# Attention followed by two MoE layers on one core: the products with V one slot later, and a unit's outputs in the softmax's tiles

## The chip, the cores and the metric

The kernel runs on one core of one Trainium2 chip. The metric is device microseconds of that core for one execution of the whole program, the median of several runs. The core's engines each work through their own list of instructions in order: PE (matrix products, into the PSUM accumulators), DVE (vector operations), ACT (activation functions and copies), POOL (a second, slower vector engine) and SP (which here only issues DMAs). Semaphores hold an instruction back until what it reads is there and what it overwrites is no longer needed.

## The reference

```python
scores = scale * np.matmul(q, k.transpose(0, 1, 3, 2))        # 4 batches, 8 heads, 576 x 576, head size 64
...
h = np.maximum(x @ w1 + b1, 0.0)                              # x[i, j] = log1p(|i - j|) / log1p(max(i, 1))
bias = h @ w2                                                 # one 576 x 576 table for each head
scores = scores + bias.transpose(2, 0, 1)[None, :, :, :]
scores = scores - np.max(scores, axis=-1, keepdims=True)
attn = np.exp(scores)
attn = attn / (np.sum(attn, axis=-1, keepdims=True) + 1e-09)
return np.matmul(attn, v).astype(np.float32)
...
h = np.maximum(np.maximum(x @ w1, x @ w2), x @ w3)            # first MoE: 2304 tokens, 512 -> 768
return (h @ w_out).astype(np.float32)                         # 768 -> 512
...
g = np.where(pos, h, np.where(neg, 0.0, (h + beta) ** 2 / (4.0 * beta)))   # second MoE: h = x @ w_in, 512 -> 2048
return (g @ w_out).astype(np.float32)                         # 2048 -> 512
```

## The kernel before

**Attention in slots.** The 576 query rows are cut into four blocks of 128 and a rest of 64. A *unit* is one block of one batch: eight heads, so eight *slots*; the rest block takes two heads at once and has four slots a unit. There are 20 units and 144 slots. Blocks 0, 1 and 2 come first, four units each (slots 0 to 95); then, for each batch, a unit of block 3 and one of the rest block (slots 96 to 143).

**One slot.** `emit_s` (L664) computes scores on PE, two slots together; the two tiles tagged `s` are PSUM. `emit_soft` takes them: DVE adds the bias table and finds the row maximum in one instruction (L678, into a tile tagged `sp`), ACT takes the exponential (L680, in place), ACT copies it to 16 bits (L696, the first half of a tile tagged `phl`), POOL computes what the rounding lost (L697 and L698, the second half), and a transposing DMA on SP's queue (L700) writes both halves, turned, into a tile tagged `pt`. `emit_pv` (L716 for the rest block, L720 otherwise) multiplies the turned probabilities with V, 14 products a slot, into the accumulator `pav`. (In the first two units every odd slot is turned on PE instead, L683 to L692.)

**The lag.** The main loop goes over slots i and emits the score of slot i + 1, the softmax of slot i and the product with V of slot i - LAG. LAG is read with `PRM.get("lag", 3)`.

**A unit's end.** After its last product `emit_norm` scales the accumulator by the sums (DVE L732, into `xf`, of which there is one), copies it to 16 bits (ACT L734, into `px`, of which there is one), computes the rest (POOL L735) and turns it by a DMA (L743) into `xT`, from which the first MoE layer reads. `xf` also serves the bias table's first part at the start (L410).

**Tiles.** `st(shape, type, tag)` gives the next tile of a tag's ring; a tag has the number of tiles that BUFS and `bufs` say (`sp` 4, `phl` 4, `pt` 4, `k` 5), and whoever gets a tile again waits for its last readers.

**What stands around it.** PE's other work fills the gaps between slots: the bias tables of the next blocks (L375 and L356), the first MoE layer (`mlp1` L775, three products of 12 matmuls for one of its columns, and `mlp2` L797), and sums that scale the weights (L454, L522). Everything is recorded with a priority, and a scheduler orders each engine's list from these priorities and from its own estimate of times; no list is written out by hand. After the last slot come the rest of the first MoE layer, and from about 660 us on the second one (L1007 and L1033, L1085 and L1124).

Of the kernel before, what the change touches and what calls it, by code (L numbers as in the profile page):

```python
# [7 lines left out]
F16 = mybir.dt.float16  # L8
BF16 = mybir.dt.bfloat16
F32 = mybir.dt.float32  # L10
# [10 lines left out]
def kernel(ctx: ExitStack, tc: tile.TileContext, qt, kt, vr, small, mw1, mw2, mw3, mwo, win, wo2, out):  # L21
# [8 lines left out]
    P = 128  # L30
    B, H, S, D = 4, 8, 576, 64
# [12 lines left out]
        ef=1,  # L44
        vl=[0, 0, 2, 11],
        vm=[0, 0, 8, 15],
        vs=[0, 0, 11, 19],
        wo=38,
        cm=[0, 3, 6, 9, 13, 16],
        veng='vv',  # L50
# [13 lines left out]
        look=4,  # L64
        xat=1,
        xs=12,
        bufs={'k': 5, 'pt': 4, 'xT': 2, 'phl': 4},
        xeng='vvvv',
        b1='vg',
        cs=8,  # L70
        cr=1,
    )
    WO, VENG, WENG, PENG, WARM, WARM2 = (PRM[k] for k in ("wo", "veng", "weng", "peng", "warm", "warm2"))
# [20 lines left out]
    def st(shape, dt, tag):  # L94
        return sb.tile(shape, dt, tag=tag, name=tag, bufs=BUFS.get(tag, 1))
# [69 lines left out]
    if True:  # L165
# [91 lines left out]
        for g in range(4):  # L257
            p = slice(32 * g, 32 * g + 32)
# [136 lines left out]
        def bias_pair(gq):  # L395

            pb = ps.tile([P, 2, 512], F32, tag="s", name="s", bufs=2)
            for c in range(2):
                m = st([P, 2 * S], F16, "phl")[:, :8 * P].rearrange("p (t i) -> p t i", t=8)
                w0 = rw[:, S - 4 * (8 * (gq + c) + 7):][:, 0:P]  # L400
                win_ = bass.AP(tensor=w0.tensor, offset=w0.offset, ap=[w0.ap[0], [4, 8], [1, P]])
                V.tensor_tensor(m, win_, thr[:, 0:P].unsqueeze(1).to_broadcast([P, 8, P]), ALU.is_gt)
                pbc = pb[:, c].rearrange("p (x q g) -> p x q g", x=16, q=8)
                for t in range(8):
                    for s in range(2):
                        T.matmul(pbc[:, :, 7 - t], m[:, t], coef[:, s].rearrange("p a h g -> p (a h) g"), start=(s == 0), stop=(s == 1))
            pbv = pb.rearrange("p c (a h k) -> p c a h k", a=2, h=H)
            k = slice(32 * gq, 32 * gq + 64)
            tmp = st([P, 512], F32, "xf").rearrange("p (c h k) -> p c h k", c=2, h=H)
            V.tensor_tensor(tmp, pbv[:, :, 0], xt0[:, k].rearrange("p (c k) -> p c k", c=2).unsqueeze(2).to_broadcast([P, 2, H, 32]), ALU.mult)  # L410
            for c in range(2):
                last_pair[0] = V.scalar_tensor_tensor(bias_sb[0][:, :, 32 * (gq + c):32 * (gq + c) + 32], pbv[:, c, 1], c_cs, tmp[:, c], ALU.mult, ALU.add)
# [312 lines left out]
        def emit_norm(u):  # L725
            n = u.n
            m = 64 * n
            rd = st([P, H, 1], F32, "rd")
            V.tensor_scalar(rd[:, :n, 0], u.sums[:, :n], 1e-9, None, ALU.add)
            V.reciprocal(rd[:, :n, 0], rd[:, :n, 0])  # L730
            xf = st([P, 512], F32, "xf")
            V.tensor_tensor(xf[:, :m].rearrange("p (h d) -> p h d", h=n), u.pav[:, :m].rearrange("p (h d) -> p h d", h=n), rd[:, :n].to_broadcast([P, n, 64]), ALU.mult)  # L732
            px = st([P, 1024], F16, "px")
            A.activation(px[:, :m], xf[:, :m], AF.Copy)  # L734
            G.tensor_tensor(px[:, m:2 * m], xf[:, :m], px[:, :m], ALU.subtract)  # L735
            key = (u.j, 0 if n == 4 else u.b // 2)
            if key not in xbox:
                xbox[key] = st([P, 2048], F16, "xT")
            if n == 4:
                d = xbox[key].rearrange("p (c b t) -> p c b t", c=4, b=B)[:, :, u.b]  # L740
            else:
                d = xbox[key].rearrange("p (c t) -> p c t", c=8)[:, :, P * (u.b % 2):P * (u.b % 2) + P]
            SP.dma_start_transpose(out=d, in_=px[:, :2 * m])  # L743
# [114 lines left out]
        for gq in range(0, 18, 2):  # L858
            bias_pair(gq)
            while conv_left and PRM["cm"][6 - len(conv_left)] <= gq - 18:  # L860
                conv_moe(conv_left.pop(0))
# [32 lines left out]
        for i in range(NS + LAG + 1):  # L894
# [15 lines left out]
            with sooner("norm"):  # L910
                while pend_norm:
                    emit_norm(pend_norm.pop(0))
# [51 lines left out]
        with sooner("norm"):  # L964
            while pend_norm:
                emit_norm(pend_norm.pop(0))
# [249 lines left out]
```

## Time and profile before

| | |
|---|---|
| median of 3 runs | 1042.64 us (1042.3 to 1043.9) |
| the profiled execution | 1048.62 us, of which the span of its instructions is 1046.9 us |
| mean granted clock of PE | 0.942 |
| busy share of the span | PE 90%, PE's weight loads 74%, DVE 68%, ACT 57%, POOL 48% |
| the chain that ended last | PE 51%, DVE 16%, DMA 12%, ACT 9%, POOL 5% |
| products with V | from 50.6 us to 583.2 us |

An idle engine costs time only where somebody waits for it. PE has the largest share, so its idle stretches, and what ended them, are the first thing to read; the trace puts in brackets how long an engine sat idle before an instruction and who released it. The granted clock is 1 at 2.4 GHz and one half at 1.2 GHz; a value between them is a mean over a stretch with both.

### The profile page before, as it was taken

Reading aid. Unit: us, or ns where it says so; the run is one execution under the profiler, and the core shown is the slowest. Engines: PE = TensorE matmul, PEld = TensorE weight load, DVE = VectorE, ACT = ScalarE, POOL = GpSimd, SP = SyncE. Lnnn points to the kernel's source line nnn. Section 1 sums busy time; section 2 is a strip of 40 time slices with the busy share of each in tenths; the row PEclk is TensorE's granted clock in tenths of the full one; section 3 lists DMA queues with packets and bytes.
Section 4 is the critical chain, followed back from the end, with each engine's and each line's share of the span. In section 5 each row is a group of like instructions: output and inputs, shape, how many; then the busy total and the mean of one; then the engine's idle time right before and its main releaser. Section 6 shows DMA issues by size and latency. Waiting matters only on the chain.

```text
span 1046.9 us, 25962 instructions
## 1 busy us (share of the span) xinstructions
PE 946.7 (90%) x10258; PEld 769.7 (74%) x10258; DVE 713.8 (68%) x1614; ACT 600.0 (57%) x1194; POOL 498.4 (48%) x721
## 2 busy tenths in 40 slices
PE   5669788898999999998899889989999999999993
PEld 5547667677888878877677768534588888888882
DVE  8977777776556678654455487598786677676662
ACT  4688874864565645777677677443344444344441
POOL 1012477665667764655455221986034344344340
PEclk7667889989999999999999899999999999999997
DMA  9795998998799988999999842010020010000000
GB/s 302 218 264 124 243 209 216 195 211 216 158 242 195 191 189 183 214 237 213 201 217 182 205 169 92 21 41 1 1 82 22 1 41 22 2 21 21 2 22 20
DMA packets 238910, 141.47 MB, mean 135 GB/s; under 512 B 187460, under 2 KB 217668, under 8 KB 238276
## 3 DMA queue, kind: packets, MB, share of 16 engines
q1 hardware_dynamic: 238788, 139.81, 57.0%
q8 instruction: 80, 1.31, 0.5%
q14 instruction: 42, 0.34, 0.1%
HBM read 79.68 MB, written 15.27 MB: 91 GB/s over the span
## 4 chain that ended last, share of the span: by engine, by line
PE 51%; DVE 16%; DMA 12%; ACT 9%; POOL 5%; issue 5%; SPq 1%; POOLq 0%; DVEq 0%; ACTq 0%
PE pm L1085 13%; PE pm L775 12%; PE s L1124 11%; DMA pt<-phl 5%; PE s L664 5%; PE pav L720 3%; PE s L1033 2%; PE pm L797 2%; POOL phl L698 2%; ACT sp L680 2%; DVE sp L678 2%; PE pm L375 1%; DMA x_d<-hl 1%; DMA ab<-in_moe_w_dram 1%; ACT phl L696 1%
## 5 line engine op out<-in xcount | busy, mean ns | idle before, releaser
L775 PE MATMUL pm<-xT,aw 128*128 128x256 f16 (+1 forms) x2160 | 246.6, 269 | 9.6 <-ACT hm L780 4.3
L775 PEld LDWEIGHTS <-aw 128*128 128x128 f16 x2160 | 194.0, 101 | 47.0 <-issue 25.4
L698 POOL TENSOR_TENSOR phl<-sp,phl 128x512 f16<-128x512 f32 x136 | 161.7, 1189 | 0.0
L680 ACT ACTIVATE sp<-sp,mx 128x576 f32<-128x576 f32 x144 | 110.6, 768 | 79.3 <-DVE mx L678 79.1
L664 PE MATMUL s<-k,qz 64*128 64x288 f32 (+1 forms) x576 | 134.8, 455 | 11.1 <-DVE mx L678 8.7
L697 POOL TENSOR_TENSOR phl<-sp,phl 128x64 f16<-128x64 f32 x136 | 48.4, 356 | 200.4 <-ACT phl L696 128.4
L1102 ACT ACTIVATE sp<-pm,vec 128x256 f32<-128x256 f32 x112 | 61.3, 556 | 93.5 <-PE pm L1085 93.4
L678 DVE CUSTOM_DVE_ANT_0 sp<-s,ab 128x576 f32<-128x576 f32 x128 | 93.7, 752 | 30.1 <-POOL phl L698 11.7
L720 PEld LDWEIGHTS <-pt 128*128 128x128 f16 x1792 | 75.9, 102 | 36.7 <-DMA pt<-phl 22.7
L664 PEld LDWEIGHTS s<-k,qz 64*128 64x128 f32 (+1 forms) x576 | 72.6, 198 | 33.2 <-DVE mx L678 13.0
L696 ACT ACTIVATE phl<-sp 128x576 f16<-128x576 f32 x136 | 89.9, 672 | 2.4 <-DMA pt<-phl 1.7
L720 PE MATMUL pav<-v,pt 128*128 128x64 f16 x1568 | 73.8, 198 | 17.6 <-DMA pt<-phl 15.8
L1085 PEld LDWEIGHTS <-ab 128*128 128x128 f16 x840 | 82.1, 98 | 10.3
L797 PE MATMUL pm<-hh,wo 128*128 128x256 f16 x648 | 78.4, 276 | 4.5 <-ACT hl L802 3.4
L1106 POOL TENSOR_TENSOR hh<-hh 128x128 f32<-128x128 f32 x56 | 30.3, 540 | 106.2 <-DVE hh L1104 101.3
L1103 DVE SCALAR_TENSOR_TENSOR hh<-pm,vec,sp 128x256 f32<-128x256 f32 x112 | 52.7, 478 | 34.3 <-ACT sp L1102 34.1
L797 PEld LDWEIGHTS <-wo 128*128 128x128 f16 x648 | 62.6, 99 | 15.3 <-issue 6.0
L787 POOL TENSOR_TENSOR hh<-hm,hh 128x256 f16<-128x256 f32 (+1 forms) x60 | 43.7, 728 | 63.3 <-ACT hh L786 62.0
L782 DVE SCALAR_TENSOR_TENSOR hm<-pm,hm 128x256 f32<-128x256 f32 (+1 forms) x120 | 47.1, 392 | 36.0 <-PE pm L775 19.1
L1124 PEld LDWEIGHTS <-xT 128*128 128x128 f16 x588 | 57.4, 98 | 7.8 <-ACT xT L1111 1.2
L1124 PEld LDWEIGHTS <-wo 128*128 128x128 f16 x588 | 57.5, 98 | 6.7
L1107 POOL TENSOR_TENSOR hh<-hh 128x128 f32<-128x128 f32 x56 | 25.8, 461 | 72.6 <-DVE hh L1104 67.9
(282 smaller groups left out, 1945.5 us busy)
## 6 DMA issues: line engine op xcount, KB each, us to landing
k<-in_k_dram SPq DMA_DIRECT2D x64, 288.0 KB, 4.1
v<-v_d SPq DMA_DIRECT2D x24, 640.0 KB, 4.9
ws<-in_moe_w_out_dram SPq DMA_DIRECT2D x15, 512.0 KB, 5.6
ws<-in_moe_w_in_dram SPq DMA_DIRECT2D x11, 512.0 KB, 4.4
x_d<-hl SPq DMA_DIRECT2D x36, 128.0 KB, 2.8
qz<-in_q_dram SPq DMA_DIRECT2D x16, 256.0 KB, 4.8
ab<-in_moe_w_dram SPq DMA_DIRECT2D x8, 512.0 KB, 8.8
qz<-x_d SPq DMA_DIRECT2D x4, 1024.0 KB, 4.8
```

The costliest lines, as they stand in the source:

```text
L664: last_score[0] = T.matmul(sbox[i + r][:, c, :288], q[p, s if u.j == SJ else s // 2], k[p, 288 * c:288 * c + 288], start=True, stop=True)
L678: V.tensor_tensor_reduce(halves(sn), sbox.pop(i)[:, :, :288], halves(bias_sb[u.j][:, h]), -0.125, 3e38, ALU.add, ALU.min, mx)
L680: last_soft[0] = A.activation(pf, sn, AF.Exp, scale=-1.0, bias=mx, accum_out=u.sums[:, h:h + 1])
L696: A.activation(hl[:, :S], pf, AF.Copy)
L698: G.tensor_tensor(hl[:, S + 64:], pf[:, :512], hl[:, :512], ALU.subtract)
L720: T.matmul(u.pav[:, 64 * h:64 * h + 64], pt[:, c], v[:, sl, 64 * (h % 4):64 * (h % 4) + 64], **kw)
L775: T.matmul(o, wm[:, ft, i, wp, kk], x_rhs(key, xp, kk) if n == 256 else x_rhs(key, xp, kk)[:, c], start=(x == 0), stop=(x == 11))
L797: T.matmul(pm, wo16[:, ft, wp, P * d:P * d + P], hh[:, ft, hp], start=(ft == 0 and y == 0), stop=(ft == NF1 - 1 and y == 2))
L1085: T.matmul(pm, w[:, wp, kk], x2t[ORDER[y]][:, kk, xp, 256 * sub:256 * sub + 256], start=(x == 0), stop=(x == 11))
L1102: A.activation(r, pm, AF.Relu, scale=c_ch[:, f], bias=c_half)
L1103: V.scalar_tensor_tensor(t, pm, c_c[:, f], r, ALU.mult, ALU.max)
L1124: T.matmul(m[x], gl[:, gp, i], w[:, wp], start=(start and z == 0 and x % 2 == 0), stop=(stop and z == 2 and (x % 2 == 1 or x == 6)))
```

## The change

The products with V are emitted four slots behind the softmax (`lag=4`). The ring of turned probabilities has five tiles instead of four, and so has `phl`. `xf` and `px` are gone: a unit's scaled outputs take the next `sp` tile, their 16-bit halves the next `phl` tile, and the bias table's first part takes an `sp` tile for its temporary. The split of batch 3's V (`vs`) moves from slot 19 to slot 20, since it overwrites what the product of slot 15 reads. No instruction is added or removed on any engine. A line of PRM is added, so every line after the 71st of the kernel before has a number that is greater by one.

```diff
-        vs=[0, 0, 11, 19],
+        vs=[0, 0, 11, 20],
...
-        bufs={'k': 5, 'pt': 4, 'xT': 2, 'phl': 4},
+        bufs={'k': 5, 'pt': 5, 'xT': 2, 'phl': 5},
...
         cs=8,
+        lag=4,
         cr=1,
...
-            tmp = st([P, 512], F32, "xf").rearrange("p (c h k) -> p c h k", c=2, h=H)
+            tmp = st([P, S], F32, "sp")[:, :512].rearrange("p (c h k) -> p c h k", c=2, h=H)
...
-            xf = st([P, 512], F32, "xf")
+            xf = st([P, S], F32, "sp")
...
-            px = st([P, 1024], F16, "px")
+            px = st([P, 2 * S], F16, "phl")
```

**PE, slot 124** (the first slot of block 3, batch 2). Before: the scores of slots 124 and 125 (`s_8862`, `s_8863`), then the products of slots 120 to 124, each shown by its first weight load (`pt_8670`, `pt_8728`, `pt_8784`, `pt_8876`, `pt_8940`), and the scores of slots 126 and 128 between them.

```order
L664 MATMUL s_8862<-k_8657,qz_67 128x288
L664 MATMUL s_8863<-k_8657,qz_67 128x288
...
L720 LDWEIGHTS pt_8670
...
L720 LDWEIGHTS pt_8728
...
L664 MATMUL s_8980<-k_8774,qz_67 128x288
...
L720 LDWEIGHTS pt_8784
...
L720 LDWEIGHTS pt_8876
...
L664 MATMUL s_9093<-k_8429,qz_67 128x288 x2
L720 LDWEIGHTS pt_8940
```

After: the scores of slots 124 and 125 (`s_8786`, `s_8787`), then the products of slots 119 to 124 (`pt_8529` to `pt_8868`), with the scores of slots 126 and 128 between them.

```order
L665 MATMUL s_8786<-k_8589,qz_67 128x288
L665 MATMUL s_8787<-k_8589,qz_67 128x288
...
L717 LDWEIGHTS pt_8529
...
L665 MATMUL s_8918<-k_8716,qz_67 128x288 x2
...
L721 LDWEIGHTS pt_8602
...
L721 LDWEIGHTS pt_8672
...
L721 LDWEIGHTS pt_8726
...
L665 MATMUL s_9051<-k_8385,qz_67 128x288 x2
L721 LDWEIGHTS pt_8800
...
L721 LDWEIGHTS pt_8868
```

Between a slot's score and its own product stood the products of four other slots; now there are five.

**PE, slot 111** (the fourth slot of block 3, batch 1). Before: the scores of slots 110 and 111 (`s_8044`, `s_8045`), then the products of slots 106 to 111 (`pt_7842` to `pt_8172`).

```order
L664 MATMUL s_8044<-k_7829,qz_67 128x288
L664 MATMUL s_8045<-k_7829,qz_67 128x288
...
L716 LDWEIGHTS pt_7842
...
L716 LDWEIGHTS pt_7916
...
L664 MATMUL s_8158<-k_7971,qz_67 128x288
...
L720 LDWEIGHTS pt_7984
...
L720 LDWEIGHTS pt_8058
...
L664 MATMUL s_8287<-k_8102,qz_67 128x288
...
L720 LDWEIGHTS pt_8112
...
L720 LDWEIGHTS pt_8172
```

After: the score of slot 111 (`s_7987`), then the products of slots 105 to 111 (`pt_7727` to `pt_8114`).

```order
L665 MATMUL s_7987<-k_7767,qz_67 128x288 x2
...
L717 LDWEIGHTS pt_7727
...
L717 LDWEIGHTS pt_7780
...
L665 MATMUL s_8100<-k_7904,qz_67 128x288
...
L717 LDWEIGHTS pt_7864
...
L665 MATMUL s_8245<-k_8046,qz_67 128x288 x2
L721 LDWEIGHTS pt_7917
...
L721 LDWEIGHTS pt_8000
...
L721 LDWEIGHTS pt_8056
...
L721 LDWEIGHTS pt_8114
```

One product more stands between score and product here too, but the last four products now follow each other with no other matmul of PE between them.

**DVE, the end of the unit of the rest block, batch 1** (slots 116 to 119). Before: the scaled outputs go to `xf_8881`, between the softmax of slots 123 (`sp_8868`) and 124 (`sp_8932`).

```order
L678 ISA sp_8868,mx_8869<-s_8715,ab_65 128x576
L678 ISA mx_8869 128x1
L159 SCALAR_TENSOR_TENSOR ab_65<-sp_8604,vec_70,ab_65 128x512
L782 SCALAR_TENSOR_TENSOR hm_68<-pm_8730,hm_68 128x256
L732 TENSOR_TENSOR xf_8881<-pav_8628,rd_8878 128x256
L803 TENSOR_REDUCE vec_70<-hl_8805 128x1
L803 TENSOR_REDUCE vec_70<-hl_8829 128x1
L678 ISA sp_8932,mx_8933<-s_8862,ab_65 128x576
```

After: they go to `sp_8873`, between the softmax of slots 124 (`sp_8860`) and 125 (`sp_8924`).

```order
L679 ISA sp_8860,mx_8861<-s_8786,ab_65 128x576
L679 ISA mx_8861 128x1
L804 TENSOR_REDUCE vec_70<-hl_8821 128x1
L733 TENSOR_TENSOR sp_8873<-pav_8629,rd_8870 128x256
L679 ISA sp_8924,mx_8925<-s_8787,ab_65 128x576
L679 ISA mx_8925 128x1
L804 TENSOR_REDUCE vec_70<-hl_8898 128x1
L679 ISA sp_8972,mx_8973<-s_8918,ab_65 128x576
```

The outputs now stand one slot later in DVE's list, and they take a turn in the ring of four that the softmax uses.

## Rows read from the trace of the kernel before

**Rows 1.** Stretches: length, busy PE, PEld, DVE, ACT, POOL; clock, DMA share, GB/s.

```profile
300.00:350.00 50.00, 49.78 (x704) 42.54 (x702) 30.23 (x72) 30.23 (x76) 35.61 (x47) 1.00 1.04 215
...
450.00:500.00 50.00, 46.42 (x590) 36.52 (x589) 28.08 (x76) 40.05 (x86) 29.04 (x43) 0.97 1.11 229
500.00:550.00 50.00, 45.60 (x577) 36.34 (x575) 25.54 (x63) 35.32 (x78) 24.90 (x34) 0.97 0.97 203
```

**Rows 2.** Waits of PE, whole span: us in total, times, longest us.

```profile
PE pav L720 <- DMA pt<-phl: 18.6, 10, 3.2
PE s L664 <- DVE mx L678: 8.7, 8, 3.0
...
PE pav L716 <- DMA pt<-phl: 4.0, 2, 3.0
```

**Rows 3.** Timeline of PE, products with V after a wait: start, us, instructions, [idle before].

```profile
75.90 1.68 PE L720 MATMUL pav<-v,pt 128*128 128x64 f16 x28 [3.17 <-DMA pt<-phl]
...
164.46 0.58 PE L720 MATMUL pav<-wo,pt 128*128 128x64 f16 x14 [2.82 <-DMA pt<-phl]
194.40 0.58 PE L720 MATMUL pav<-v,pt 128*128 128x64 f16 x14 [2.54 <-DMA pt<-phl]
209.89 0.93 PE L720 MATMUL pav<-v,pt 128*128 128x64 f16 x14 [2.36 <-DMA pt<-phl]
...
474.45 0.49 PE L720 MATMUL pav<-v,pt 128*128 128x64 f16 x11 [2.22 <-DMA pt<-phl]
522.77 0.58 PE L720 MATMUL pav<-v,pt 128*128 128x64 f16 x14 [3.22 <-DMA pt<-phl]
...
582.49 0.96 PE L716 MATMUL pav<-v,pt 128*64 128x64 f16 x28 [2.96 <-DMA pt<-phl]
```

**Rows 4.** Two stretches of 10 us with such a wait, columns as in rows 1.

```profile
470.00:480.00 10.00, 7.78 (x85) 6.11 (x85) 4.12 (x14) 6.70 (x16) 4.94 (x7) 0.83 1.17 268
...
520.00:530.00 10.00, 7.23 (x67) 6.00 (x68) 5.28 (x14) 7.31 (x17) 3.56 (x6) 0.83 1.07 258
```

**Rows 5.** Timeline of PE: what its matmuls take.

```profile
153.38 0.63 PE L375 MATMUL pm<-coef,masks 128*128 128x64 f16 x16
155.07 0.83 PE L775 MATMUL pm<-xT,aw 128*128 128x128 f16 x12
...
475.01 2.26 PE L775 MATMUL pm<-xT,aw 128*128 128x256 f16 x13
...
506.98 1.24 PE L664 MATMUL s<-k,qz 64*128 64x288 f32 x8
510.74 2.13 PE L797 MATMUL pm<-hh,wo 128*128 128x256 f16 x18
512.70 0.57 PE L720 MATMUL pav<-v,pt 128*128 128x64 f16 x14
514.38 1.48 PE L775 MATMUL pm<-xT,aw 128*128 128x256 f16 x12
```

**Rows 6.** Timeline, a unit's outputs and what follows, 507 to 518 us.

```profile
507.96 0.63 ACT L734 ACTIVATE px<-xf 128x512 f16<-128x512 f32 x1 [3.81 <-DMA xT<-px]
509.86 0.42 DVE L732 TENSOR_TENSOR xf<-pav,rd 128x256 f32<-128x256 f32 x1 [6.63 <-POOL px L735]
512.99 0.42 ACT L734 ACTIVATE px<-xf 128x256 f16<-128x256 f32 x1 [3.36 <-DMA xT<-px]
517.02 1.42 SPq L700 DMA_TRANSPOSE pt<-phl  x1
```

**Rows 7.** Timeline, ACT near the last slot.

```profile
570.73 0.42 ACT L734 ACTIVATE px<-xf 128x256 f16<-128x256 f32 x1 [1.16 <-DMA xT<-px]
```

**Rows 8.** Waits of DVE, whole span, columns as in rows 2.

```profile
DVE sp L678 <- POOL phl L698: 11.7, 12, 3.2
```

**Rows 9.** The page's groups: line, operation, count | busy, mean ns | idle before.

```profile
L698 POOL TENSOR_TENSOR phl<-sp,phl 128x512 f16<-128x512 f32 x136 | 161.7, 1189 | 0.0
```

**Rows 10.** DMA issues: count, median us from issue to landing.

```profile
pt<-phl SPq DMA_TRANSPOSE x136, 4.5
```

## The prediction

> **What bounds the kernel now.** I began with the table of stretches [rows 1], because a share over the whole span hides where an engine is free. From 300 to 350 us PE is busy for 49.78 of 50 us at full clock; from 450 to 550 us it is busy for 92.0 of 100 us (46.42 + 45.60) and the clock is 0.97. No other engine comes near that: the next in [rows 1] is ACT with 40.05 of 50. So PE sets the time, and what can be won is its idle time and the stretches at the low clock. Next I read whom PE waits for [rows 2]: turned probabilities are late 12 times, for 18.6 + 4.0 = 22.6 us. This is the wait that a greater lag aims at, and no other line of [rows 2] is half as large. Then the timeline, for where these waits stand [rows 3]: three lie between 164 and 210 us, one at 474, one at 523, the last one at the very end of attention. From 210 to 474 us [rows 3] has none (a single one of 0.15 us is left out), which is why 300 to 350 us is so full: the lag of three is already enough there.
>
> What such a wait costs beyond itself is seen in [rows 4] and [rows 5]: in the 10 us around the waits at 474 and 523 us the granted clock is 0.83, and 13 matmuls right after the first took 2.26 us at the low level (1.2 GHz), against 12 in 1.48 us later at the high one (2.4 GHz). 13 at the high level would be 1.60, so 0.66 us is lost at least; 0.17 of 10 us is 1.7 at most. I take the middle, 1.2 us for each wait that goes.
>
> **What the order says of each wait.** No operation is added or removed, so no busy time changes; all depends on where a slot's product stands behind its score. I counted the PE work between the two in each order, at the durations of [rows 5] (a pair of scores 1.24, a product with V 0.57, twelve matmuls of the first MoE 1.48 or 0.83, eighteen of `mlp2` 2.13, sixteen of a bias table 0.63; the rest block's products and the few other matmuls at some tenths): an estimate of how long softmax and DMA may take before PE waits.
> - On average over slots 48 to 95 it grows from 21 to 25 us, over slots 96 to 143 from 14.7 to 17.4. Over slots 0 to 35 it stays at 15.8: there the scheduler had mostly put a product five to nine scores behind already. So the change bites from about 210 us on, and most of that stretch had no wait.
> - Slot 124 (the wait of 3.22 at 523 us): 11.7 to 19.5. It goes, for a second reason too [rows 6]. ACT sat idle for 3.81 and 3.36 us because the one `px` was still being turned; between them DVE sat idle for 6.63 because the one `xf` was still being read. The softmax of slots 124 and 125 was queued behind these on DVE and then on ACT, and slot 124's DMA was issued at 517.02 only. With `sp` and `phl` tiles neither wait stands. Gain 3.22 + 1.2 = 4.4.
> - Slot 30 (2.82 at 164 us): 14.6 to 19.1. The wait goes, but behind it PE works on bias tables that ACT, POOL and DVE must drain in turn before new scores may run, and they may set that stretch instead. Gain between 0 and 2.82 + 1.2; I take half, 2.0.
> - Slot 33 (2.54 at 194 us): 33.2 to 36.0. It is the second slot after all had waited for block 1's table. More MoE work stands before slot 33's product now and less before the next ones, so the wait is moved on: 0.
> - Slot 38 (2.36 at 210 us): 9.2 to 8.1. Less stands between than before: 1.1 us lost.
> - Slot 111 (2.22 at 474 us): 11.4 both times, since the last products before it follow each other bare. Nothing is won: 0.
> - Slots 4 and 5 (3.17 at 76 us): about 1 us more stands between. The waits for the maximum (8.7 us in [rows 2]) belong to the same softmax, so I count nothing (at best 1.2).
> - The last slot (2.96 at 582 us): 9.1 to 9.7, so 0.6; and ACT's wait of 1.16 for `px` [rows 7], which stands ahead of the last exponential, goes; I count half. Gain 1.2, at best 1.8.
>
> **The shared tiles.** A unit's outputs now take one of the four `sp` tiles, and the next softmaxes find a ring that is one tile shorter until POOL has read the outputs. In the trace DVE already waits for POOL to free an `sp` tile 12 times, 11.7 us in all [rows 8]. DVE's wait holds back the scores' tiles and so PE: 8.7 us in [rows 2], most of it early. The nearest price of one more such wait is one POOL subtraction, 1.19 us [rows 9]. If none reaches PE it costs nothing, and since the removed waits on `xf` are counted above it gains nothing either; if all 20 outputs bring one that reaches PE it is 23.8 us. With products a slot later the softmax has more room, so I take the low end: 1.0. The fifth `phl` tile is a fair exchange: an output holds one while it is turned (its cover: nine users in eight slots, five tiles), and if that cover fails, ACT's copy waits for a landing of about 4.5 us [rows 10] and the DMAs queued behind on SP with it. The split of batch 3's V one slot later has eight slots of room until its first use, so I cost it at nothing; without that room it would be one V load, about a landing. The temporary of the first bias table is written and read on DVE alone in its list's order: nothing.
>
> **Sum.** -4.4 - 2.0 + 1.1 - 1.2 + 1.0 = -5.5 us. The profiled execution took 1048.62 us, 1.7 more than its span and 6.0 more than the median of 1042.64; the terms are stretches of it that I expect in every execution. So 1043.1 for a profiled run and 1037.1 for the median.
>
> **The rivals.**
> - *All waits go.* The six waits of [rows 3] before the last are 16.3 us; with 1.2 each for the clock and 1.2 at the end this is 24.7 us: 1018. For it: each wait is shorter than the slot that is added (attention's 144 slots take 533 us, 3.7 each). Against it: the counts at slots 33, 38 and 111.
> - *Nothing moves, DMA sets the pace.* The DMA engines' busy share is 1.04 to 1.11 in stretches of [rows 1], and 1.17 at the wait at 474 us [rows 4]. If transposes can't come faster, a slot of room is used up once and the waits come back: 1042.6, and up to 2 us either way. Against it: from 300 to 350 us the share is 1.04 and PE does not wait. The Trainium skill, Perfetto Trace Analysis, section Identifying the Most-Contended Engine, says that occupancy misleads for the 16 DMA engines and wants the HBM utilization read; by that rule this rival falls, and the 300 to 350 us stretch agrees; by occupancy alone the gain would be 0.
> - *Slower: the shared ring.* DVE waits for an `sp` tile at the softmax behind an output, the scores' tiles stay taken, and PE waits at L665. Each costs 1.19 us; against the 6.5 us that the other terms give it decides from six of the 20 outputs on. With half of them, 10, it is 11.9 - 6.5 = 5.4 slower: 1048. For it: the 12 waits of [rows 8]. Against it: DVE is busy for only 25 to 30 of 50 us in [rows 1].
>
> **How the numbers follow.** The forecast has a chance of 0.50 (its own range 1031 to 1042), all waits going 0.10, no change 0.18, the ring 0.22. A difference of 0.2%, about 2 us, is what a measurement of this kernel can tell from none. Faster: 0.45 of the forecast and the 0.10, 0.55. Same: 0.05 of the forecast, 0.15 of the second rival and 0.02 of the third, 0.22. Slower: 0.23. The range from 1026 to 1049 leaves out the far half of the first rival and the outer part of the ring's bound.
>
> **What would show it.** Right: no wait of PE on `pt` near slot 124; ACT and DVE with no wait on a unit's outputs; waits on `pt` still there after block 1's table (190 to 215 us) and near slot 111; in all about 15 us of such waits instead of 22.6. Wrong: DVE waiting for POOL at L679 for much more than 11.7 us with PE waiting at L665 behind it; or new waits on `pt` as long as the old ones between 210 and 460 us.

## The result and the profile after

The changed kernel takes 1057.6 us (median of 4 runs, 1055.4 to 1065.1); the kernel before took 1042.8 beside it. The ratio is 1.0144, 95% interval 1.0115 to 1.0174: some 15 us slower. The forecast was 1037, in a range from 1026 to 1049.

Most of the waits that the change aims at are gone. PE's waits in the kernel after, as in [rows 2] (line numbers from L72 on are one higher than before):

```profile
PE s L665 <- DVE mx L679: 14.6, 12, 3.2
PE pav L721 <- DMA pt<-phl: 6.4, 2, 5.0
...
PE pav L717 <- DMA pt<-phl: 2.8, 1, 2.8
```

The waits for turned probabilities fell from 22.6 us in 12 to 9.2 in 3. The timeline of PE shows where the three stand, as in [rows 3]; all that stood between 190 and 580 us are gone:

```profile
80.43 0.93 PE L721 MATMUL pav<-v,pt 128*128 128x64 f16 x14 [4.99 <-DMA pt<-phl]
...
170.63 0.58 PE L721 MATMUL pav<-wo,pt 128*128 128x64 f16 x14 [1.45 <-DMA pt<-phl]
...
588.88 0.96 PE L717 MATMUL pav<-v,pt 128*64 128x64 f16 x28 [2.82 <-DMA pt<-phl]
```

The stretches of [rows 1] are fuller too, and the granted clock from 450 to 500 us is 1.00 instead of 0.97:

```profile
300.00:350.00 50.00, 50.00 (x674) 42.46 (x672) 29.54 (x69) 29.85 (x72) 33.02 (x44) 1.00 1.04 210
450.00:500.00 50.00, 49.95 (x596) 39.86 (x594) 29.10 (x72) 39.86 (x86) 28.29 (x42) 1.00 1.13 236
500.00:550.00 50.00, 46.03 (x581) 36.15 (x581) 26.77 (x63) 37.29 (x81) 25.89 (x36) 0.97 1.06 217
```

But look at the first of them: PE is busy for all of 50 us and ran 674 matmuls, where it ran 704 before. A busier PE did less: the 56 score matmuls on 64 rows in that stretch take 9.9 us (8.7 before), and 32 fewer matmuls of bias tables fit. So the next view is the page's first lines, the span and PE's busy time. Before:

```profile
span 1046.9 us, 25962 instructions
...
PE 946.7 (90%) x10258; PEld 769.7 (74%) x10258; DVE 713.8 (68%) x1614; ACT 600.0 (57%) x1194; POOL 498.4 (48%) x721
```

After:

```profile
span 1063.3 us, 26004 instructions
...
PE 966.5 (91%) x10258; PEld 779.0 (73%) x10258; DVE 721.3 (68%) x1614; ACT 604.3 (57%) x1194; POOL 502.5 (47%) x721
```

The same 10258 matmuls take 19.8 us more; PE's idle time (span less busy) is 96.8 us after and 100.2 before. So the span's 16.4 us are 19.8 of busy time less 3.4 of idle time: of the 13.4 us of waits that went, 10 came back as others, such as the waits for the maximum (8.7 to 14.6). (Both profiled executions are longer than their medians, by 7.5 us after and by 6.0 us before, so their difference of 16.4 us is near the medians' 14.7.)

Groups of PE by line with each shape apart (count | busy, mean ns | idle before), before:

```profile
L664 PE MATMUL s<-k,qz 64*128 64x288 f32 x512 | 114.7, 457 | 11.1 <-DVE mx L678 8.7 <-DVE vec L142 1.0 <-PE s L406 0.6
L664 PE MATMUL s<-k,qz 128*128 128x288 f32 x64 | 20.1, 438 | 0.0
```

After:

```profile
L665 PE MATMUL s<-k,qz 64*128 64x288 f32 x512 | 134.6, 478 | 17.4 <-DVE mx L679 14.2 <-issue 2.3 <-PE s L407 0.4
L665 PE MATMUL s<-k,qz 128*128 128x288 f32 x64 | 19.5, 425 | 0.3 <-DVE mx L679 0.3
```

The 512 score matmuls on 64 rows hold PE for 19.9 us more, though one of them takes hardly longer (478 ns, 457). A mean times a count that is well above the busy time is a sign of overlap, and it is the overlap that has shrunk. The timeline shows it at slots 110 and 111, the place of the second order excerpt on PE in the section on the change. Before:

```profile
460.17 1.24 PE L664 MATMUL s<-k,qz 64*128 64x288 f32 x8
461.34 1.48 PE L775 MATMUL pm<-xT,aw 128*128 128x256 f16 x12
```

After:

```profile
464.98 1.24 PE L665 MATMUL s<-k,qz 64*128 64x288 f32 x4
466.14 0.63 PE L717 MATMUL pav<-v,pt 128*64 128x64 f16 x28
466.70 1.23 PE L665 MATMUL s<-k,qz 64*128 64x288 f32 x4
```

A pair of slots has two score halves, one on rows 0 to 63 of PE and one on rows 64 to 127. Eight matmuls that stand together take 1.24 us; four alone take 1.23. So a pair whose halves are separated by other work costs PE 1.2 us more. (The 28 products between them are one slot of the rest block, 14 for each of its two heads.) The Trainium skill, TensorE: Matmul & The Clock Gate, Part 3: Packing small matmuls — row/col tiling, says that matmuls that need fewer than 128 rows can run concurrently in the array, each at a tile position of its own; by these rows that holds here only for halves that PE finds next to each other.

In PE's order of instructions the four matmul instructions of a pair stand in one piece, the halves alternating ("together" below), for 40 of 64 pairs before and for 25 after. From slot 36 on, pairs whose halves have other work between them went from 3 to 15, and those in three pieces or with a gap from 3 to 6. The added busy time lies in these slots. The scores from slot 36 on, before (187.5 to 600 us):

```profile
L664 PE MATMUL s<-k,qz 64*128 64x288 f32 x368 | 65.1, 435 | 1.0 <-DVE mx L678 1.0
```

After (188.5 to 600 us):

```profile
L665 PE MATMUL s<-k,qz 64*128 64x288 f32 x368 | 86.5, 455 | 5.5 <-DVE mx L679 5.5
```

Of these 21.4 us, 12 more separated pairs at 1.23 us are 14.8; pairs in pieces and separated pairs at the low clock make up most of the rest. In the first 36 slots the scores take 49.7 us before and 48.1 after.

### The profile page after: what moved, and what is told of

Its sections match the earlier page's. It is cut to its first block, busy times and chain, and to the rows that moved or that the text cites. A ratio compares the mean times of both kernels' runs of the same rounds, so it can differ in the third digit from the quotient of the medians.

```text
span 1063.3 us, 26004 instructions
## 1 busy us (share of the span) xinstructions
PE 966.5 (91%) x10258; PEld 779.0 (73%) x10258; DVE 721.3 (68%) x1614; ACT 604.3 (57%) x1194; POOL 502.5 (47%) x721
## 4 chain that ended last, share of the span: by engine, by line
PE 58%; DVE 16%; ACT 9%; DMA 7%; issue 5%; POOL 3%; SPq 1%; DVEq 0%; POOLq 0%; ACTq 0%
PE pm L1086 13%; PE pm L776 12%; PE s L1125 11%; PE s L665 8%; PE pm L798 4%; PE pav L721 3%; PE s L1034 2%; PE pm L376 2%; DVE sp L679 2%; DMA v<-in_moe_w_out_dram 2%; ACT sp L681 2%; DMA ws<-in_moe_w_out_dram 1%; DMA pt<-phl 1%; DVE aw L160 1%; DMA ws<-in_moe_w_dram 1%
## 5 line engine op out<-in xcount | busy, mean ns | idle before, releaser
L665 PE MATMUL s<-k,qz 64*128 64x288 f32 (+1 forms) x576 | 154.1, 472 | 17.7 <-DVE mx L679 14.6
L679 DVE CUSTOM_DVE_ANT_0 sp<-s,ab 128x576 f32<-128x576 f32 x128 | 94.5, 751 | 48.1 <-PE s L665 34.3
L665 PEld LDWEIGHTS s<-k,qz 64*128 64x128 f32 (+1 forms) x576 | 82.8, 206 | 44.3 <-DVE mx L679 17.2
L721 PEld LDWEIGHTS <-pt 128*128 128x128 f16 x1792 | 73.6, 101 | 28.5 <-issue 13.1
L798 PE MATMUL pm<-hh,wo 128*128 128x256 f16 x648 | 82.0, 282 | 3.6 <-DVE hm L783 1.7
L721 PE MATMUL pav<-v,pt 128*128 128x64 f16 x1568 | 70.7, 197 | 7.4 <-DMA pt<-phl 5.0
```

What stands on the lines that cost most here:

```text
L665: last_score[0] = T.matmul(sbox[i + r][:, c, :288], q[p, s if u.j == SJ else s // 2], k[p, 288 * c:288 * c + 288], start=True, stop=True)
L679: V.tensor_tensor_reduce(halves(sn), sbox.pop(i)[:, :, :288], halves(bias_sb[u.j][:, h]), -0.125, 3e38, ALU.add, ALU.min, mx)
L721: T.matmul(u.pav[:, 64 * h:64 * h + 64], pt[:, c], v[:, sl, 64 * (h % 4):64 * (h % 4) + 64], **kw)
L798: T.matmul(pm, wo16[:, ft, wp, P * d:P * d + P], hh[:, ft, hp], start=(ft == 0 and y == 0), stop=(ft == NF1 - 1 and y == 2))
```

## The experiments

**Theory P:** the lag moves the two halves of a pair apart in PE's order, and that busy time is the loss. **Rival R:** the tiles that outputs and softmax now share are the loss. In the runs from e5 on **theory E:** the lag costs in the first 40 slots too, where everything waits for the first products. All runs were made beside the kernel before; 1042.8 to 1043.4 are its medians. "Lag" is in slots, up to slot 40 and from then on; PE busy, idle and busy up to 250 us are from the profiled execution; "busy of scores" is the group at L664 and its like.

| kernel | tiles | lag | pairs together | median us (range) | ratio, 95% | PE busy + idle | busy of scores | busy to 250 us |
|---|---|---|---|---|---|---|---|---|
| before | own | 3, 3 | 40 | 1042.8 | | 946.7 + 100.2 | 134.8 | 199.4 |
| e4 | own | 3, 3 | 0 | 1046.8 (1039.4-1054.0) | 1.0008-1.0080 | 943.6 + 101.7 | 135.9 | 198.3 |
| e3 | shared | 3, 3 | 40 | 1043.6 (1036.5-1052.4) | 0.9978-1.0040 | 946.7 + 102.5 | 134.6 | 198.3 |
| e8 | shared | 3, 4 | 27 | 1056.3 (1048.8-1059.3) | 1.0076-1.0148 | 961.8 + 94.9 | 150.3 | 198.7 |
| e9 | shared | 4, 3 | 33 | 1051.9 (1044.3-1058.3) | 1.0045-1.0102 | 947.6 + 101.6 | 139.0 | 198.4 |
| after | shared | 4, 4 | 25 | 1057.6 (1055.4-1065.1) | 1.0115-1.0174 | 966.5 + 96.8 | 154.1 | 196.7 |
| e12 | shared | 4, 4, fill sooner | 25 | 1058.9 (1051.1-1060.0) | 1.0101-1.0161 | 961.6 + 96.0 | 154.1 | 201.2 |
| e2 | own | 3, 3 | 61 | 1036.9 (1034.6-1044.1) | 0.9918-0.9967 | 921.0 + 113.7 | 107.9 | 188.5 |
| e5 | shared | 3, 3 | 57 | 1039.7 (1038.0-1043.2) | 0.9931-0.9989 | 923.4 + 114.7 | 110.5 | 185.5 |
| e10 | shared | 3, 3, V split later | 57 | 1038.6 (1034.7-1041.3) | 0.9928-0.9973 | 918.4 + 114.8 | 109.0 | 184.0 |
| e6 | shared | 3, 4 | 55 | 1038.5 (1035.4-1044.6) | 0.9932-0.9978 | 922.7 + 110.9 | 113.8 | 186.7 |
| e7 | shared | 4, 3 | 59 | 1053.8 (1052.1-1058.0) | 1.0073-1.0129 | 918.5 + 132.7 | 111.8 | 174.1 |
| e1 | shared | 4, 4 | 60 | 1049.1 (1046.4-1053.9) | 1.0038-1.0083 | 921.8 + 127.4 | 107.1 | 171.4 |
| e11 | shared | 4, 4, fill sooner | 56 | 1040.9 (1035.8-1045.3) | 0.9956-0.9999 | 922.5 + 118.0 | 112.9 | 179.8 |

**e1 and e2: the halves kept together, in the kernel after and in the one before.** A matmul of one column is put into the second half's PSUM tile first, so that neither half starts before both tiles are free, and the four matmuls follow each other. The edit, the same in both:

```diff
+            prev = T.matmul(sbox[i + 1][:, 0, :1], ones, ones[:, :1], start=True, stop=True) if len(rows) == 2 else None
             for c in range(2):
                 for r, p in enumerate(rows):
-                    last_score[0] = T.matmul(...)
+                    with tc.issue_after(prev.ins) if prev is not None else nullcontext():
+                        last_score[0] = T.matmul(...)
+                    prev = last_score[0]
```

> The changed kernel, with the four score matmuls of a pair held together (a one-column matmul first takes the second PSUM tile, the four follow each other in the order first half, second half, first, second): 60 of 64 pairs stand together in PE's list instead of 25. Theory P (the change is slow because its order tears the two halves of a pair apart, which then no longer run beside each other on PE, 1.23 us against 2 x 1.23): score matmuls' busy time falls from 154 to under 125 us, time 1028 to 1042 us. Rival R (the change is slow because outputs in the softmax's ring, or the greater lag itself, make DVE and PE wait): the time stays above 1052 us and the waits of PE for the maximum (14.6 us) stay. Rival C (the clock in 200 to 250 us, 0.77 instead of 0.93, is the cause): the time falls only if that clock is back, by 5 us at most.

> The kernel before, with the pairs held together in the same way: 61 of 64 pairs instead of 40 (of the 46 pairs from slot 36 on 43 instead of 39). Theory P: few pairs to win from slot 36 on (about 4 us), some in the first 36 slots where DVE is as busy as PE (0 to 15 us), and 64 small matmuls more (4 to 10 us): 1030 to 1043 us. The difference of e1 to this run is then the lag's own worth with the pairing made equal: between -12 and +3 us by theory P, +12 us or more by rival R.

Measured: e1 1049.1, 8.5 us under the kernel after; e2 1036.9, 5.9 under the kernel before, and faster than both kernels. PE by line and shape in e2, with the added matmuls (11 us of busy time, some of it beside other work):

```profile
L666 PE MATMUL s<-k,qz 64*128 64x288 f32 x512 | 87.3, 456 | 7.9 <-DVE mx L681 6.2 <-DVE ab L412 1.6
...
L662 PE MATMUL s<-ones 128*128 128x1 bf16 x64 | 10.9, 171 | 6.9 <-DVE mx L681 6.2 <-DVE ab L412 0.6
```

In e1 the first of these groups is 87.8. So e1 lies between what P gave (1028 to 1042) and what R gave (above 1052): with the halves together 8.5 us of the 15 come back. Rival C, the clock from 200 to 250 us (0.77 in the kernel after, 0.93 before), doesn't explain the loss: it is 0.93 again in e1, but e8 and e12 below have 0.84 and 0.86 there and are as slow as the kernel after, while e3 has 0.86 and is not. Busy time saved is not time won, either: e2 saves 26.9 us of the scores' busy time against before, 22.2 of them in the first 36 slots (49.7 to 27.5), but PE's idle time rises by 13.5 us and the medians differ by 5.9 only.

With the same busy time of PE (921.8, 921.0), e1 is still 12.1 us slower than e2, which P doesn't give: PE is idle for 13.7 us longer. PE's waits for the maximum and for turned probabilities in e1:

```profile
PE pav L724 <- DMA pt<-phl: 25.7, 12, 5.5
PE s L663 <- DVE mx L682: 10.0, 5, 3.9
PE s L667 <- DVE mx L682: 9.4, 9, 2.4
...
PE pav L720 <- DMA pt<-phl: 1.8, 2, 1.1
```

The waits for the maximum stay, as R said (19.4 us, 14.6 in the kernel after). And the waits for turned probabilities are back, 27.5 us in 14, more than before the change, although the lag is four. So it is not shown that the lag alone removed them in the kernel after: the scores that hold PE longer there may have a share. The two kernels' stretches say where the time is lost. e1:

```profile
0.00:250.00 250.00, 171.42 (x2557) 144.97 (x2558) 192.53 (x464) 168.93 (x348) 113.62 (x164) 0.83 0.91 223
250.00:600.00 350.00, 330.31 (x4334) 276.63 (x4331) 209.66 (x503) 226.17 (x512) 196.88 (x267) 0.98 0.94 201
```

e2:

```profile
0.00:250.00 250.00, 188.53 (x2794) 159.12 (x2795) 204.40 (x489) 175.60 (x365) 125.42 (x176) 0.85 0.92 228
250.00:600.00 350.00, 325.49 (x4214) 272.56 (x4212) 206.90 (x533) 230.53 (x519) 190.03 (x259) 0.98 0.95 203
```

By 250 us e1 has run 237 matmuls less; behind that it is not the slower one. This points to the first 250 us for the remaining 12 us; e5 to e7 test it.

**e3: the kernel after with a lag of three.** Its tiles and rings are left as in after.

```diff
-        vs=[0, 0, 11, 20],
+        vs=[0, 0, 11, 19],
-        lag=4,
+        lag=3,
```

> The changed kernel with the lag back at three and batch 3's split back at slot 19; the outputs still in the softmax's tiles, five pt and five phl tiles: 40 of 64 pairs together, as in the kernel before. Theory P: 1037 to 1048 us, score matmuls 130 to 140 us. Rival R in its form with the shared ring: 1052 us or more, as the ring is still shared; in its form with the lag itself: 1037 to 1048 too, with the waits of PE for the maximum back at about 9 us.

Measured 1043.6, no different from before, with 134.6 us of scores, as P gave. R falls in its form with the shared ring: the shared tiles and longer rings cost nothing by themselves. In its other form, in which the lag makes DVE and PE wait, it fits this run as well as P does; e8 parts the two.

**e4: the kernel before with the halves of a pair one after the other, not alternating.**

```diff
-            for c in range(2):
-                for r, p in enumerate(rows):
+            for r, p in enumerate(rows):
+                for c in range(2):
```

> The kernel before with the two halves of a pair emitted one after the other: no pair together; of the 46 pairs from slot 36 on 37 stand as first, first, second, second and 9 with other work between. Theory P: about 28 us more on PE from slot 36 on (6 pairs more apart at 1.22, 36 at 0.57), time 1060 to 1075 us, score matmuls' busy time 160 to 185 us. If the side by side running of the halves is no matter (R, C): 1040 to 1048 us.

Measured 1046.8, with 135.9 us of scores, far under what P gave, and within the 1040 to 1048 of R and C. The edit did not do what P needed, so this time speaks for neither side; why it is 4.0 us above before's, with PE no busier, is not shown. From slot 36 on, 37 pairs now have one half directly behind the other; the timeline shows one of them:

```profile
464.53 1.25 PE L664 MATMUL s<-k,qz 64*128 64x288 f32 x8
```

They overlap as alternating ones do. P was too strict: not the alternation counts, but that nothing else stands between the halves, and that the second half's PSUM tile is free in time. Where it isn't, PE waits between them; an early pair in the kernel before, with nothing else between its halves:

```profile
54.65 1.23 PE L664 MATMUL s<-k,qz 64*128 64x288 f32 x4
58.91 1.91 PE L664 MATMUL s<-k,qz 64*128 64x288 f32 x4 [3.03 <-DVE mx L678]
```

So the early pairs were mostly apart before the change too.

**e5, e6 and e7: where the lag costs, the halves kept together.** All three are e1 with another lag: three throughout (e5), three up to slot 40 and then four (e6), four and then three (e7). The edit of e6 (e7's is its mirror, with two slots' products at the change):

```diff
-            if i >= LAG and i - LAG < NS:
+            p = i - 3 if i < 40 else i - 4 if i > 40 else -1
+            if 0 <= p < NS:
```

> The kernel after with its shared tiles and bigger rings and the kept-together halves of e1, but with the products three slots behind (57 of 64 pairs stand together). e1 and e2 stand 12 us apart although their score products take the same time, and e1 is already 9 us behind e2 at its 14th softmax. Theory E (the fourth slot of lag costs those 12 us in the first 40 slots, by later products and outputs): 1037 us (1033 to 1041), as e2. Rival R (the tiles that outputs and softmax share cost them, early): 1046 to 1050, as e1.

> As e5, but the products stand three slots behind up to slot 40 and four from then on (55 pairs together). Theory E: the late part of the lag costs nothing, so 1033 to 1041, within 3 us of e5. Rival T (the fourth slot costs wherever it stands, by one more slot of fill work that comes late): 1042 to 1049. Rival R: 1046 to 1050.

> The opposite of e6: four slots behind up to slot 40, three from then on (59 pairs together). Theory E: the loss is all early, so 1046 to 1051, as e1. Rival T: about half of it, 1040 to 1046. Rival R: 1046 to 1050, not told from E here but by e5.

Measured: 1039.7, 1038.5 and 1053.8 (a little above what E gave). With the halves together, the fourth slot of lag costs nothing from slot 40 on (e6 against e5: -1.3) and 14.1 us before it (e7 against e5). E holds there; R falls again, and so does T, that the lag costs wherever it stands. Nor does the later lag win anything clear here: e6's and e5's intervals overlap, and the waits for turned probabilities are 22.1 and 23.6 us. What PE does less in the first 250 us is fill work. Groups of PE up to 250 us in e6 (first MoE layer, bias tables):

```profile
L780 PE MATMUL pm<-xT,aw 128*128 128x128 f16 (+1 forms) x576 | 50.9, 244 | 0.9 <-ACT ab L387 0.5 <-DVE ab L384 0.2
...
L377 PE MATMUL pm<-coef,masks 128*128 128x64 f16 x528 | 20.5, 196 | 1.9 <-DVE ab L384 0.8 <-DVE masks L373 0.7 <-ACT hm L785 0.2
```

In e7:

```profile
L780 PE MATMUL pm<-xT,aw 128*128 128x128 f16 (+1 forms) x518 | 41.4, 236 | 9.3 <-ACT hm L785 4.4 <-DVE hm L787 2.3 <-ACT ab L387 1.4
...
L377 PE MATMUL pm<-coef,masks 128*128 128x64 f16 x480 | 18.4, 196 | 0.7 <-DVE ab L384 0.3 <-DVE masks L373 0.2 <-ACT ab L387 0.2
```

9.5 us of the first layer and 2.1 of the bias tables are missing, of the 12.6 us by which PE's busy time up to 250 us differs.

**e8 and e9: the same switches with the halves left to the scheduler,** that is, in the kernel after.

> The kernel after, its score halves as the scheduler puts them (27 of 64 pairs together), with three slots of lag up to slot 40 and four from then on. By the pairs that e1 mended (8.5 us) and theory E (12 us early) as separate costs, the pairs' cost alone is left: 1044 to 1050. Were the separated pairs without cost, and the whole loss early, it would be 1037 to 1043; were the loss spread over the slots (T), 1050 to 1056.

> The kernel after with its score halves as the scheduler puts them (33 of 64 pairs together), four slots of lag up to slot 40 and three from then on. Early lag cost 14 us with the halves kept together (e7 against e5), late lag 13 us with them free (e8 against e3), yet both at once give only 15 in the kernel after. If the early cost stands by itself (additive): e3's 1043.6 and 11 to 14, with some for 33 pairs in place of 40: 1054 to 1060. If TensorE is filled by the separated halves early anyway, so that the early lag costs nothing there: 1043 to 1049.

e8 missed: 1056.3, not 1044 to 1050; it lies at the upper end of T's 1050 to 1056. But T's late fill work would cost with the halves together too, and e6 shows no cost there. Four runs with the same tiles and a lag of three up to slot 40 make a square. With the halves free, a lag of four from slot 40 on costs 12.7 us (e3 1043.6, e8 1056.3); with the halves together it costs nothing (e5 1039.7, e6 1038.5). So what the later lag costs is the separation of the halves: e8's scores' busy time is 15.7 us above e3's (from slot 36 on 87.3 for 70.3), while PE's idle time is 7.6 us less, which R's waits don't give. The timeline of e8 at one such pair:

```profile
462.40 1.24 PE L666 MATMUL s<-k,qz 64*128 64x288 f32 x4
463.57 0.39 PE L777 MATMUL pm<-xT,aw 128*128 128x256 f16 x2
463.89 0.63 PE L718 MATMUL pav<-v,pt 128*64 128x64 f16 x28
464.45 1.24 PE L666 MATMUL s<-k,qz 64*128 64x288 f32 x4
```

e9 came out at 1051.9, between its two answers: the early lag alone costs 8.3 us here. Its scores' busy time is 4.4 us above e3's, all in the first 36 slots (49.3 for 44.9); what that is worth in time is not shown. Both lags at once cost 13.9 (after against e3), not 21: the two losses cover each other in part.

**e10, e11 and e12: by what the early lag costs.** e10 is e5 with the late step of V's split that the kernel after needs (`vs` 20 for 19). e11 is e1, e12 the kernel after, with this edit alone:

```diff
-            while done_blocks and i >= done_blocks[0][0] + 2:
+            while done_blocks and i >= done_blocks[0][0] + 1:
                 queue_mlp(*done_blocks.pop(0)[1:])
```

> e5 with the third pass of the split of V one slot later (20 for 19), which the kernel after needs for its lag and e1 and e7 have too, e5 and e6 have not. If the lag of the products itself costs the early time: within 3 us of e5's 1039.7. If this later split does: 1046 to 1054, as e1 and e7.

> e1 (four slots of lag, halves kept together, 1049.1) with a unit's fill work of the first layer queued one slot after its last product instead of two, so that it is queued in the slot in which a lag of three has it. If the early cost is that fill work is queued a slot later: 1037 to 1042. If it is the products' and outputs' own delay, or the split of V: 1046 to 1052. Between: both have a share.

> The kernel after with e11's one edit (a unit's fill work queued one slot after its last product, not two) and nothing else: its halves stay as the scheduler puts them, 25 of 64 pairs together as in after. If the fill work queued late costs the kernel after its own share beside the separated halves, as in e11: 1048 to 1053. If that cost is covered there, since the kernel after loses only 1.3 us against e8, which has no early lag: 1055 to 1060.

All three fell into one of the ranges given. e10: 1038.6, so it isn't the split of V. e11: 1040.9, so 8.2 us of e1's come back when a unit's fill work is queued a slot sooner, which undoes what the lag does to it. PE up to 250 us in e11:

```profile
0.00:250.00 250.00, 179.78 (x2599) 148.26 (x2600) 198.45 (x470) 170.66 (x351) 114.45 (x165) 0.83 0.89 223
```

8.4 us more than e1, the same amount. e12: 1058.9, no gain. So in the kernel after the late fill work costs nothing that can be seen. The likely reason, argued and not tested, is that the separated halves cover it: with the halves free PE is busy for 197 to 201 us of the first 250 whatever the lag, and scores alone hold it for 63 to 69 us there, against 40 to 46 with the halves together. Why the 4.6 us that e12 has done more by 250 us don't shorten it is open; its busy time from 250 to 600 us is 336.8, with 13.2 idle where after has 10.2.

## Why the prediction was wrong

- **"No operation is added or removed, so no busy time changes; all depends on where a slot's product stands behind its score."** This step failed. The same matmuls took 19.8 us more, because what they cost depends on their neighbours: the scores from slot 36 on took 86.5 us for 65.1. e8 against e3 shows a lag of four from slot 40 on taking 15.7 us more of the scores' busy time and 12.7 us of time, and e6 against e5 shows that with the halves together it takes no time. The prediction had both pieces in hand: it priced "a pair of scores 1.24" from [rows 5], and the order excerpt for slot 111 shows the scores of slots 110 and 111 together before, and that of 111 alone after. It counted the room between score and product, and not what the score now cost.
- **The waits.** Slot 124's went as forecast, with ACT's waits for the transposed outputs (9.8 us before, none in the trace after). Of the two reasons given, the second was enough: e3, with the new tiles and a lag of three, has no wait at slot 124 either (0.17 us at the next slot), and is no faster than before. The waits at slots 33, 38 and 111, said to stay or grow, went too: 9.2 us of waits on `pt` are left, not 15. The rival that all waits go came nearer here than the forecast, but perhaps in part by luck: the scores held PE longer, which neither foresaw, and in e1, with the halves together, 27.5 us are left. What was mistaken was also to take a wait of PE that goes as time won: PE's idle time fell by 3.4 us only.
- **Slots 30, 4 and 5, the tail.** At slot 30 (170 us) 1.45 of 2.82 is left, where the wait was to go and half of the gain was counted; at 80 us, now at slot 6, the wait is longer than before (4.99 for 3.17, where nothing was counted; e3 has 5.84 there, so it is not the lag's); at the end it is 2.82 for 2.96, where 0.6 was to be won.
- **The shared tiles, +1.0.** e3 puts them at +0.8, which is not told from 0. DVE's waits behind POOL for an `sp` tile, 11.7 us before [rows 8], are 4.9 in the kernel after, and in e3 9.8, with 5.0 more behind POOL's reading of a unit's outputs; they cost e3 no time that can be seen. The rival that forecast a slower kernel did so by these waits; that its sign agrees with the result is luck.
- **"So the change bites from about 210 us on."** Wrong as well, though hidden in the kernel after: the lag also delays the fill work that is queued behind a unit's last product. With the halves together the early lag costs 11 to 14 us (e1 against e6, e7 against e5), and e11 gives 8.2 of it back by queueing that work a slot sooner.

What stays open: how the 15 us divide when both losses act, since they cover each other. By the medians the late lag's separated halves (12.7, with the early lag at three) leave only 1.3 for the early lag (after against e8), which the spread of the runs doesn't tell from 0. And with both losses mended, in e11, a lag of four (1040.9) is no faster than a lag of three with the halves together (1039.7 in e5, 1036.9 in e2).

## What to carry to other kernels

Before calling a reordering free of busy time, ask which instructions share the engine with a neighbour: where a group's mean time multiplied by its count is well above its busy time, it overlaps, and the order is part of its price. Compare the work done, in matmuls of the same shape, not the busy share, when PE looks full. And a software pipeline's lag moves everything that is queued behind the delayed step: here queueing the first layer's work one slot sooner gave back 8.2 us with the halves together (e11), and nothing with them apart (e12).

## What the runs showed of the hardware

- Two 64-row halves of fp32 scores overlap wholly whether their matmuls alternate (8 in 1.24 us) or one half stands directly behind the other (8 in 1.25 us, e4), though PE's list then has all of the first half ahead of the second. With 28 products with V between them they don't overlap (twice 1.24 us for 4). The Trainium skill, TensorEngine Tiling (Array Packing), Key Properties, says that a change of the tiling mode drains TensorE; work on all 128 rows between two halves would be such a change, but no run here tells that apart from the order alone.
- A matmul of one column takes PE 0.17 us (64 of them, 10.9 us in e2).
